# Retention attention and an ELU feed-forward on one core: chunks of 64 tokens on 64x64 quads, with keys and values re-laid by DMA, in place of chunks of 128 tokens kept two tokens to a partition

## The chip, the core and the metric

The kernel runs on one core of a Trainium2 chip. The metric is the device time of one execution, in microseconds (us). The profile is of one execution and gives the span from the first to the last instruction, which is a little shorter than the device time.

The core has a matrix engine (PE in the profile, with its weight loads shown apart as PEld), a vector engine (DVE), a scalar engine (ACT), a third elementwise engine (POOL), and a queue processor (SP) that here only issues DMAs. PE multiplies a stationary block (at most 128 by 128) with a moving block of up to 512 columns and writes into PSUM, which has eight banks of 512 fp32 columns. POOL does not read PSUM in this kernel. Three queues can issue DMAs: SP's, POOL's and ACT's.

## What is computed

The inputs are `q`, `k` and `v` (8 batches, 8 heads, 576 tokens, 64 values a head, fp32) and two weights of 512 by 2048 and 2048 by 512. Attention is linear with a decay in place of a softmax, so that it can be computed in chunks with a running state. What follows is a feed-forward network (FFN) on all 4608 tokens.

```python
scores = scale * np.matmul(q, k.transpose(0, 1, 3, 2))
gamma = 1.0 - 2.0 ** (-5.0 - np.arange(H, dtype=np.float32))
rel = pos[:, None] - pos[None, :]
Dmat = np.where(rel >= 0, gamma[:, None, None] ** rel[None, :, :], 0.0)
attn = np.matmul(scores * Dmat, v)            # 8 batches, 8 heads, 576 x 64
x = attn.transpose(0, 2, 1, 3).reshape(B * S, H * D)      # 4608 x 512
h = x @ w_in                                              # 4608 x 2048
g = np.where(h > 0.0, h, np.exp(np.minimum(h, 0.0)) - 1.0)
out = g @ w_out                                           # 4608 x 512
```

## The kernel before

**Decay and chunks.** The decay `gamma ** (i - j)` splits into a factor on the queries and one on the keys (`gq`, `gk`, scaled copies made by `scaled` at L427). Inside a chunk the scores are multiplied by a 0/1 mask; what earlier chunks contribute comes from a state, the sum of `k^T v` over them, kept per head pair as a block-diagonal 128x128 matrix.

**Attention items.** There are 36 items. A main item is 256 tokens of one batch and 4 heads (two items, `w` = 0 and 1, for each batch and each of two `T`), so 32 of them; a tail item holds the last 64 tokens of two batches with all 8 heads, and there are 4 of these. A main item loads q, k and v with 256 KB each, as pairs of neighbouring tokens in one partition (`(p e) d -> p h (e d)`, packets of 512 B). A chunk of a main item is 128 tokens: 64 partitions with two parities `e`. So keys never have to be moved: `do_scores` (L547) makes a 128x128 score block a head out of 64x64 matmuls with 128 columns, in four quadrants of the array at once ("quads"), and `do_values` and `do_state` sum over the two parities.

**From load to x.** For each main item: POOL or DVE scale q and k (four instructions of 128x256), POOL or ACT cast v; q and k are transposed, by PE for the first seven items (`turn_pe`, L449, `PE_TURN = 7`) and after that by a DMA transpose on SP's queue (L491); PE makes scores; DVE multiplies them by the mask (L673, 128x1024); PE adds the values and the part from the states into two banks; ACT or DVE copy these into `xt`, the input of the FFN. The states go from PSUM to `mid` and `end` (L630 to L639, DVE) and POOL spreads them over the block diagonal (L647).

**How PE runs attention.** The first items run in separate pieces (`early`, `early_out`). Then one "stretch" (L738) puts the state part of the previous item, the scores of this one, the values of the previous one and the states of this one behind one another. A stretch reserves two of the six banks of class `f` (`reserve`, L729); the score tile has two banks of its own (`sc`).

**FFN.** It works in 18 blocks of 256 tokens. FFN1 (`ffn1`, L801) fills one bank with 8 matmuls of 256 columns; ACT takes the exponential, DVE (or ACT) the middle step, DVE makes `g`. FFN2 (`ffn2`, L853) sums 16 matmuls of 512 columns into one bank for 128 tokens; ACT copies it and SP stores it. FFN1 of one block is interleaved with FFN2 of the block before.

**The order of the work** is made when the program is built: `Plan` (L35) is a list scheduler with a cost for every step, with slots for tiles and banks, and with a model of the DMA queues. Each engine executes its steps in the order that the plan gives. `rank` is the priority, and `LEAD = 64` puts attention four blocks ahead of the FFN. The weights come by POOL's queue, cast to bf16 on the way, in four pieces each (L406, L414).

Of the kernel before, what the change touches and what calls it, by code (L numbers as in the profile page):

```python
# [22 lines left out]
class Op:  # L23


    def __init__(self, name, cost, deps, emit, rank, take=(), use=(), banks=(), dma=None, after=None):
# [5 lines left out]
        self.slot, self.waits = {}, []  # L32


class Plan:  # L35
# [30 lines left out]
    def run(self, began):  # L66
# [29 lines left out]
        def pick(e, now):  # L96
            best = None
            for op in ready[e]:
                if best is not None and best[0] <= op.rank:
                    continue  # L100
# [12 lines left out]
                if got is not None:  # L113
                    best = op.rank, op, got
            return best
# [5 lines left out]
        for e, t in began.items():  # L121
            heapq.heappush(events, (t, next(count), None))
        now = 0.0
        while len(order) < len(self.ops) or any(wire.values()) or events:
# [37 lines left out]
            heads = {e: h for e, h in heads.items() if h[3] or big in ([], [e])}  # L162
# [23 lines left out]
ENTER, LEAVE = 1.25, 0.55  # L186


LEAD = 64
HOLD = {}  # L190
RANKS = {}
TOGETHER = 1
EARLY = 5
LOOSE = True
LASTB = 15
ORDER = (0, 1, 2, "t0", 3, "t1", 4, 5, 6, "t2", 7, "t3")
PE_TURN = 7
WG = ("ck11", "ck11", "ck11", "ck12")
WOG = ("ck13", "ck13", "ck13", "ck13")
FREE = ("f", "e", "em", "g", "ot")  # L200

SLOTS = {
    "f": 6, "sc": 1,
    "rqk": 8, "rv": 8, "qkn": 5, "vn": 6, "qkT": 5, "pt": 3,
    "rqt": 4, "rvt": 2, "qkt": 4, "vt": 2, "qkTt": 4, "ptt": 2,
    "xt": 5, "g": 20, "e": 4, "em": 4, "ot": 5, "mid": 4, "end": 4, "s_mid": 4, "s_end": 16,
# [4 lines left out]
def kernel(  # L211
# [15 lines left out]
    FT = 4  # L227
    ST = 64
    NU = FT + 1
    KJ = DM // P  # L230
    NFT = DF // P
    TB = 256
    NP = NFT // 2
    MID = S // 2
    C = 64
    assert (DM, S, D, HP) == (H * D, FT * P + ST, 64, KJ)

# [19 lines left out]
    for h in range(H):  # L257
        nc.vector.memset(lgt[:, h : h + 1], lg[h])
    pos_i = const.tile([P, NU], I32, name="pos_i")
    nc.gpsimd.iota(pos_i[:, :FT].rearrange("p (t e) -> p t e", e=2), pattern=[[2 * P, 2], [1, 2]], base=-MID,  # L260
                   channel_multiplier=2)
    nc.gpsimd.iota(pos_i[:ST, FT:], pattern=[[0, 1]], base=FT * P - MID, channel_multiplier=1)
    nc.gpsimd.iota(pos_i[ST:, FT:], pattern=[[0, 1]], base=MID - FT * P, channel_multiplier=-1)
    pos = const.tile([P, NU], FP32, name="pos")
# [5 lines left out]
    bt = const.tile([P, 1], FP32, name="bt")  # L270
    nc.vector.memset(bt[:ST], math.log(scale))
    nc.vector.memset(bt[ST:], 0.0)
    expo = const.tile([P, NU, H], FP32, name="expo")
    nc.vector.tensor_tensor(
        expo,
        pos.unsqueeze(2).to_broadcast([P, NU, H]),
        lgt.unsqueeze(1).to_broadcast([P, NU, H]),
        ALU.mult,
    )
    gq = const.tile([P, NU, H], FP32, name="gq")  # L280
    nc.scalar.activation(gq[:, :FT], expo[:, :FT], AF.Exp, bias=bq)
    nc.scalar.activation(gq[:, FT], expo[:, FT], AF.Exp, bias=bt)
    gk = const.tile([P, FT, H], FP32, name="gk")
    nc.scalar.activation(gk, expo[:, :FT], AF.Exp, bias=bk, scale=-1.0)

    mask = const.tile([P, 2, 2, C], BF16, name="mask")
    nc.vector.memset(mask, 1.0)
    for c in range(2):
        for ek in range(2):
            for eq in range(2):  # L290
                m = mask[c * C : (c + 1) * C, ek, eq]
                nc.gpsimd.affine_select(out=m, in_=m, compare_op=ALU.is_ge, fill=0.0, base=eq - ek,
                                        pattern=[[2, C]], channel_multiplier=-2)
    mask_t = const.tile([P, ST], BF16, name="mask_t")
    nc.vector.memset(mask_t, 1.0)
    for c in range(2):
        m = mask_t[c * ST : (c + 1) * ST]
        nc.gpsimd.affine_select(out=m, in_=m, compare_op=ALU.is_ge, fill=0.0, base=0, pattern=[[1, ST]],
                                channel_multiplier=-1)
    diag = const.tile([P, 2], FP32, name="diag")  # L300
    nc.gpsimd.memset(diag, 0.0)
    nc.gpsimd.memset(diag[:D, :1], 1.0)
    nc.gpsimd.memset(diag[D:, 1:], 1.0)
# [3 lines left out]

    plan = Plan(SLOTS)  # L310
# [8 lines left out]
    holds, chain = [], {}  # L319
# [4 lines left out]
    items = []  # L324
    for b in ORDER:
        for r in range(FT if isinstance(b, int) else 1):
            it = Item()
            it.tail = not isinstance(b, int)
            if it.tail:
                it.half = int(b[1]) % 2  # L330
                it.b, it.blk = 2 * int(b[1]), "AB"[int(b[1]) // 2]
            else:
                it.b, it.T, it.w = b, r // 2, r % 2
                it.blk = 2 * b + it.T
            items.append(it)
    for n, it in enumerate(items):
        it.n = n
        it.early = n < FT
    at = {(it.b, it.T, it.w): it for it in items if not it.tail}

    seq = list(range(2 * B))
    seq = [*seq[:B], "A", *seq[B:LASTB], "B", *seq[LASTB:]]
    place = {blk: i for i, blk in enumerate(seq)}
    for it in items:
        it.rank = it.n * 4 - 64 if it.early else place[it.blk] * 16 - LEAD + 6 * (it.half if it.tail else it.w)

    def load_main(it, srcs="qkv"):
        n = it.n  # L350
        if not hasattr(it, "ld"):
            it.ld = {}
# [68 lines left out]
    def scaled(it, i, e, cost):  # L421
# [8 lines left out]
        if first:  # L430
            it.cq = {}
# [562 lines left out]
```

## Time and profile before

| | us |
|---|---|
| device time, 3 runs | 309.63, 310.08, 311.87 |
| device time, median | 310.08 |
| span of the profiled execution | 307.9 |
| PE busy | 294.6 (96%) |
| DVE, ACT, POOL busy | 218.0, 153.4, 148.3 |
| FFN1 matmuls, 1152 with 256 columns: busy | 147.5 |
| FFN2 matmuls, 546 with 512 columns (30 more are not in the records): busy | 138.0 |
| mask on DVE, 32 with 128x1024: busy, mean of one | 38.9, 1.215 |

The span of 307.9 us and the median of 310.08 us differ by 2.2 us, which is what an execution spends outside its first and last instruction; this is taken as fixed below. A time in the profile counts from the first instruction. "Busy" is the time in which at least one instruction of a group was under way; since matmuls overlap in the pipeline, the cost of one is read from the distance of two starts and not from its own duration. An entry such as `f<-xt,w_in_sb` names the tile written and the tiles read. A "releaser" is what ended the idle time ahead of an instruction.

### The profile page before, as it was taken

Reading aid. Unit: us, or ns where it says so; the run is one execution under the profiler, and the core shown is the slowest. Engines: PE = TensorE matmul, PEld = TensorE weight load, DVE = VectorE, ACT = ScalarE, POOL = GpSimd, SP = SyncE. Lnnn points to the kernel's source line nnn. Section 1 sums busy time; section 2 is a strip of 40 time slices with the busy share of each in tenths; the row PEclk is TensorE's granted clock in tenths of the full one; section 3 lists DMA queues with packets and bytes.
Section 4 is the critical chain, followed back from the end, with each engine's and each line's share of the span. In section 5 each row is a group of like instructions: output and inputs, shape, how many; then the busy total and the mean of one; then the engine's idle time right before and its main releaser. Section 6 shows DMA issues by size and latency. Waiting matters only on the chain.

```text
span 307.9 us, 8903 instructions
## 1 busy us (share of the span) xinstructions
PE 294.6 (96%) x3600; PEld 207.0 (67%) x3647; DVE 218.0 (71%) x395; ACT 153.4 (50%) x297; POOL 148.3 (48%) x258
## 2 busy tenths in 40 slices
PE   7789999999999999999999999999999999999995
PEld 3576747767677676676676676667776666666654
DVE  4997835887687878888778787667676666666650
ACT  3467815565556645554545545345446343444431
POOL 5983469958876779988776775003011000000000
PEclk9999999999999999999999999999999999999999
DMA  6999999999999999999999998101011010000122
GB/s 198 271 216 216 216 270 256 263 249 211 247 231 211 217 247 277 243 247 305 247 214 212 274 221 151 36 35 38 34 36 36 35 36 34 36 34 34 39 56 78
DMA packets 103768, 50.12 MB, mean 163 GB/s; under 512 B 45744, under 2 KB 99248, under 8 KB 103728
## 3 DMA queue, kind: packets, MB, share of 16 engines
q1 hardware_dynamic: 99504, 45.37, 69.9%
q0 software_dynamic: 4224, 4.19, 8.0%
q8 instruction: 28, 0.46, 0.6%
q14 instruction: 12, 0.10, 0.1%
HBM read 36.70 MB, written 9.44 MB: 150 GB/s over the span
## 4 chain that ended last, share of the span: by engine, by line
PE 86%; DMA 10%; issue 2%; DVE 1%; POOL 1%; ACT 0%
PE f L245 81%; DMA rqk<-in_q_dram 6%; DMA rqk<-in_k_dram 4%; PE sc L245 3%; PE f L455 1%; POOL qkn L427 0%; PE f L953 0%; DVE qkT L461 0%; POOL s_end L647 0%; DVE qkn L427 0%; ACT ot L872 0%; DVE s_end L647 0%; DVE zero L250 0%; DVE end L639 0%
## 5 line engine op out<-in xcount | busy, mean ns | idle before, releaser
L245 PE MATMUL f<-xt,w_in_sb 128*128 128x256 bf16 x1152 | 147.5, 273 | 0.1
L245 PE MATMUL f<-w_out_sb,g 128*128 128x512 bf16 (+1 forms) x546 | 138.0, 373 | 4.3 <-issue 3.0
L817 ACT ACTIVATE e<-f 128x512 f32<-128x512 f32 x144 | 86.0, 597 | 109.2 <-PE f L245 107.5
L245 PEld LDWEIGHTS <-w_in_sb 128*128 128x128 bf16 x1152 | 111.5, 98 | 38.0
L831 DVE TENSOR_SCALAR em<-e 128x512 bf16<-128x512 f32 x105 | 53.3, 508 | 49.9 <-ACT e L817 49.3
L245 PEld LDWEIGHTS <-g 128*128 128x128 bf16 x592 | 56.0, 98 | 39.4
L841 DVE SCALAR_TENSOR_TENSOR g<-f,em 128x512 bf16<-128x512 f32 x105 | 72.2, 688 | 9.1 <-DVE em L831 0.5
L647 POOL TENSOR_TENSOR s_mid<-mid,diag 128x256 bf16<-128x256 f32 x32 | 20.0, 624 | 51.2 <-ACT mid L630 24.6
L427 POOL TENSOR_TENSOR qkn<-rqk,gq 128x256 bf16<-128x256 f32 x61 | 37.6, 632 | 11.6 <-DMA rqk<-in_q_dram 7.6
L427 POOL TENSOR_TENSOR qkn<-rqk,gk 128x256 bf16<-128x256 f32 x59 | 38.4, 667 | 5.3 <-DMA rqk<-in_k_dram 5.1
L673 DVE TENSOR_TENSOR pt<-sc,mask 128x1024 bf16<-128x1024 f32 x32 | 38.9, 1215 | 1.7 <-PE sc L245 1.7
L839 DVE SCALAR_TENSOR_TENSOR g<-e,f 128x512 bf16<-128x512 f32 x39 | 26.1, 682 | 6.0 <-ACT f L827 6.0
L872 ACT COPY ot<-f 128x512 f32<-128x512 f32 (+1 forms) x36 | 20.6, 575 | 17.8 <-PE f L245 17.7
L708 ACT CAST xt<-f 128x256 bf16<-128x256 f32 x50 | 20.0, 450 | 10.8 <-PE f L245 10.2
L827 ACT ACTIVATE f<-f 128x512 f32<-128x512 f32 x36 | 21.4, 595 | 0.0
L443 POOL CAST vn<-rv 128x512 bf16<-128x512 f32 x28 | 17.6, 629 | 7.4 <-DMA rv<-in_v_dram 7.3
L647 POOL TENSOR_TENSOR s_end<-end,diag 128x256 bf16<-128x256 f32 x28 | 17.4, 623 | 4.2 <-DVE end L639 2.7
L245 PE MATMUL sc<-qkT 64*64 64x128 bf16 x512 | 13.4, 222 | 1.7 <-DVE qkT L461 1.6
L245 PE MATMUL f<-pt,vn 64*64 64x128 bf16 x512 | 12.7, 217 | 0.0
L245 PEld LDWEIGHTS <-qkT 64*64 64x64 bf16 x512 | 8.2, 106 | 5.4 <-DVE qkT L461 2.2
L506 POOL TENSOR_TENSOR qkt<-rqt,gq 128x256 bf16<-128x256 f32 x16 | 9.9, 638 | 3.0 <-DMA rqt<-in_k_dram 3.0
L461 DVE COPY qkT<-f 128x512 bf16<-128x512 bf16 x11 | 4.6, 421 | 9.4 <-PE f L455 9.4
(65 smaller groups left out, 139.4 us busy)
## 6 DMA issues: line engine op xcount, KB each, us to landing
rqk<-in_q_dram SPq DMA_DIRECT2D x32, 256.0 KB, 5.1
rqk<-in_k_dram SPq DMA_DIRECT2D x32, 256.0 KB, 5.2
rv<-in_v_dram SPq DMA_DIRECT2D x32, 256.0 KB, 5.0
out_dram<-ot SPq DMA_DIRECT2D x31, 256.0 KB, 3.7
w_in_sb<-in_moe_w_in_dram POOLq DMA_DIRECT2D x4, 512.0 KB, 12.6
w_out_sb<-in_moe_w_out_dram POOLq DMA_DIRECT2D x4, 512.0 KB, 19.3
out_dram<-ot SPq DMA_DIRECT2D x10, 128.0 KB, 2.4
rqt<-in_q_dram SPq DMA_DIRECT2D x8, 128.0 KB, 4.0
```

What stands on the lines that cost most here:

```text
L245: pin(nc.tensor.matmul(*a, **kw))
L427: pin(alu[op.eng].tensor_tensor(tiles[key][:, i, e], tiles[raw][:, :, e], g, ALU.mult))
L443: pin(copy[op.eng](tiles["vn", n], tiles["rv", n]))
L647: pin(alu[op.eng].tensor_tensor(tiles[key].rearrange("p h (j d) -> p h j d", j=2), tiles[src].unsqueeze(2).to_broadcast([P, 2, 2, D]), dia ...
L673: pin(nc.vector.tensor_tensor(tiles["pt", n].rearrange("p i h n -> p (i h) n"), tiles["sc", n].rearrange("p i (h n) -> p (i h) n", h=2), m ...
L708: pin(copy[op.eng](dst, src))
L817: pin(nc.scalar.activation(tiles[ekey], tiles[hkey], AF.Exp))
L827: pin(nc.scalar.activation(ph, ph, AF.Relu))
L831: pin(alu[op.eng].tensor_scalar_add(em, e, -1.0))
L839: pin(nc.vector.scalar_tensor_tensor(g, e, -1.0, ph, ALU.add, ALU.min))
L841: pin(nc.vector.scalar_tensor_tensor(g, ph, 0.0, tiles["em", blk, p], ALU.max, ALU.min))
L872: pin(copy[op.eng](tiles[okey][:, :width], tiles[pkey][:, :width]))
```

## The change

The attention part is built anew, and the FFN's blocks are made wider. The scheduler gets an earliest time for a step (`early`), a `gate` on reservations, and lets ACT's queue run beside POOL's.

- A main item is 256 tokens of one batch with all 8 heads, so 16 of them; a tail item is 64 tokens of four batches, so 2. Chunks have 64 tokens. q, k and v still come as pairs of tokens; after scaling and casting into a staging tile `kvs`, two DMAs an item (`re0`, `re1`, 256 KB each) lay keys and values out again as one token a partition (`kvn`). For the first three items ACT's queue issues them, after that SP's.
- Scores, values and states are 64x64 matmuls with 64 columns, 32 of each an item. The state part has 16 matmuls an item, 128x128 with 64 columns.
- The first five items (40 heads x 256 tokens; before: the first seven, 28 heads x 256 tokens) are transposed by PE; from there on q goes by one DMA transpose and k by two, these after the re-laying.
- All eight PSUM banks are of class `f`. A stretch reserves six of them: two for scores, two for x, two for states. Masks are two of 128x512 an item; states are summed one after another over four chunks (128x256) and put on the block diagonal by two copies each into a ring of zeroed tiles.
- FFN: four blocks with 256 tokens, then seven with 512, so that FFN1 has 448 matmuls with 512 columns and 256 with 256. The weights come in 9 pieces (the first two of `w_in` half as large), at times written down in `AT`.

```diff
-LEAD = 64
-EARLY = 5
-PE_TURN = 7
-WG = ("ck11", "ck11", "ck11", "ck12")
-WOG = ("ck13", "ck13", "ck13", "ck13")
+SW_ENTER = 4.4
+LEAD = 96
+EARLY = 5
+ACT_LAY = 3
+PE_TURN = 5
+AT = {"wi0": 9.6, "wi1": 10.4, "wi2": 11.2, "wi3": 13.0, "wi4": 15.0, "wo0": 17.0, "wo1": 19.0, "wo2": 22.0, "wo3": 25.0}
+NBD = 8
+SURE = 3
+ATT = ((0, 0), (0, 1), (1, 0), (1, 1), (2, 0), (2, 1), (3, 0), (3, 1), (4, 0), (4, 1), "X",
+       (5, 0), (5, 1), (6, 0), (6, 1), (7, 0), (7, 1), "Y")
+FFN = (((0, 0),), ((0, 1),), ((1, 0),), ((1, 1),), ((2, 0), (2, 1)), ((3, 0), (3, 1)), ((4, 0), (4, 1)),
+       ((5, 0), (5, 1)), ((6, 0), (6, 1)), ("X", "Y"), ((7, 0), (7, 1)))
+W_IN = ((0, 1), (1, 2), (2, 4), (4, 6), (6, 8))
...
-    "f": 6, "sc": 1,
+    "f": 8, "rq": 3, "rk": 3, "rv": 3, "qn": 3, "kvs": 3, "kvn": 3, "qT": 3, "kT": 3, "pt": 2,
+    "xt": 4, "g": 33, "e": 4, "em": 4, "ot": 5, "S": 4,
...
+        for s in range(2):
+            def emit(op, s=s):
+                eng = nc.scalar if op.eng == "ACT" else nc.sync
+                pin(eng.dma_start(tiles[nkey][:, s].rearrange("p i h d -> p (i h d)"),
+                                  tiles[skey][s * C : (s + 1) * C].rearrange("p e i n -> p e (i n)")))
...
+            op = add(f"re{s}_{n}", {"ACT": 0.5} if n < ACT_LAY else {"SP": 0.5}, [*it.ck.values(), *it.cv], emit,
+                     it.rank if n < ACT_LAY else -1, use=[skey, *use], dma=(0.75, 8), **kw)
...
+                for s in range(2):
+                    def emit(op, tkey=tkey, s=s):
+                        pin(nc.sync.dma_start_transpose(tiles[tkey][:, s],
+                                                        tiles[nkey][:, s, 0].rearrange("p h d -> p (h d)")))
...
+    def do_scores(it):
+        kt = tiles["kT", it.n]
+        for hp in range(HP):
+            for s in range(2):
+                for par in range(2):
+                    for i in range(2):
+                        part = slice(i * D, (i + 1) * D)
+                        sc = tiles["sc", it.n, i].rearrange("p (h s n) -> p h s n", h=HP, s=2)
+                        mm(pairs(sc[rows(par), hp, s]), kt[part, s, hp, rows(par)], queries(it, part, hp, s, par),
+                           start=True, stop=True)
...
+    def do_inter(it, xkey):
+        for s in range(2):
+            for par in range(2):
+                state = state_of(it, 2 * s + par)
+                if state is not None:
+                    for hp in range(HP):
+                        acc((xkey, par), 2, pairs(quad(xkey, par, s, hp)), tiles[state][:, hp],
+                            queries(it, slice(0, P), hp, s, par))
...
+        def gate():
+            if any(r.start is not None for r in mine):
+                return True
+            free = sum(old is None or plan.left[old] == 0 for old in plan.slots["f"])
+            return free >= len(keys) or any(
+                f[0].start is not None and sum(x.start is None and all(d.done is not None for d in x.deps) for x in f) >= SURE
+                for f in tilesof2)
...
+        st = add(f"A{it.n if it else 'last'}", {"PE": cost}, deps, emit, (it or prev).rank - 4, use=use)
+        reserve(st, ([("sc", it.n, i) for i in range(2)] if it else []) + (banks_of(xkey) if prev else [])
+                + (banks_of(tkey) if it and not it.tail else []))
...
-    def ffn1(blk, p, rank):
+    def ffn1(blk, p, rank, after):
+        per, first = 512 // blk.w, blk.i < 2
+        fts = range(per * p, per * (p + 1))
...
+            for f, ft in enumerate(fts):
                 for j in range(KJ):
-                    mm(ph[:, f * TB : (f + 1) * TB], w_in_sb[:, j, ft * P : (ft + 1) * P], xt[:, j],
+                    mm(ph[:, f * blk.w : (f + 1) * blk.w], w_in_sb[:, j, ft * P : (ft + 1) * P], xt[:, j],
                        start=(j == 0), stop=(j == KJ - 1))
```

The deps of a stretch are the masks, the states and the re-laid tiles of the previous item, and the transposed and re-laid tiles of this one. For the first five items `early` runs scores, states and outputs as three separate pieces.

## The prediction

> **What bounds the kernel now.** I read the page's busy slices first, then the chain, then busy times by stage, then single stretches of PE's timeline.
>
> ```profile
> PE   7789999999999999999999999999999999999995
> ...
> DMA  6999999999999999999999998101011010000122
> ```
> ```profile
> 18.76:47.17 28.41, 26.80 (x297) 18.97 (x292) 19.83 (x37) 17.44 (x35) 15.10 (x26) 1.00 1.20 233
> 47.17:304.50 257.33, 253.00 (x3043) 178.63 (x3085) 184.42 (x316) 127.60 (x246) 118.14 (x195) 1.00 0.73 152
> ```
>
> The slices are 7.7 us each: PE is full from the fourth on, DMA only up to the 25th. The second view has stretch, length, then busy time of PE, PEld, DVE, ACT and POOL, clock, DMA share and GB/s. The first FFN1 matmul starts at 18.76 us, the last FFN2 matmul ends at 304.5. Between them PE is the bound at a granted clock of 1.00; DVE has 72% of the long stage, ACT 50%. "PE 86%" in the chain says the same. So time comes off only as PE work, or as the head before 18.76 us.
>
> What PE's time consists of is read from starts:
>
> ```profile
> 257.45 1.04 PE L245 MATMUL f<-xt,w_in_sb 128*128 128x256 bf16 x8
> 258.33 1.03 PE L245 MATMUL f<-w_out_sb,g 128*128 128x512 bf16 x4
> 259.19 1.04 PE L245 MATMUL f<-xt,w_in_sb 128*128 128x256 bf16 x8
> ```
>
> Eight FFN1 matmuls take 0.875 us (109.4 ns each), four FFN2 matmuls 0.865 (216 ns each; starts to another digit are from the same records). The whole FFN is 1152 x 0.1094 + 576 x 0.2163 = 250.6 us, of the 285.7 between 18.76 and 304.5. The other 35 us are attention and a little idle time. Two stretches of attention:
>
> ```profile
> 85.92 0.40 PE L245 MATMUL f<-qkTt,s_end 128*128 128x64 bf16 x8
> 86.25 0.42 PE L245 MATMUL sc<-qkT 64*64 64x128 bf16 x16
> 86.50 0.29 PE L245 MATMUL f<-ptt,vt 64*64 64x64 bf16 x16
> 86.62 0.30 PE L245 MATMUL f<-vn,qkn 64*64 64x64 bf16 x16
> 86.86 0.39 PE L245 MATMUL f<-xt,w_in_sb 128*128 128x256 bf16 x2
> ```
> ```profile
> 117.51 0.28 PE L245 MATMUL f<-qkT,s_mid 128*128 128x128 bf16 x2
> 117.71 0.42 PE L245 MATMUL sc<-qkT 64*64 64x128 bf16 x16
> 117.96 0.39 PE L245 MATMUL f<-pt,vn 64*64 64x128 bf16 x16
> 118.18 0.29 PE L245 MATMUL f<-vn,qkn 64*64 64x64 bf16 x16
> 118.41 0.83 PE L245 MATMUL f<-xt,w_in_sb 128*128 128x256 bf16 x6
> ```
>
> Sixteen quad matmuls take 0.25 us with 128 columns and 0.12 with 64. A 128x128 matmul with 64 columns starts every 0.029 us (inside the 85.92 group). Each stretch also pays some 0.09 us on entering the quads and 0.12 on leaving. A stretch is 0.90 us with two state matmuls; two more, at 56 ns each, make 1.01; a tail's is 0.80 (105.34 to 106.14).
>
> **The change, part by part.**
>
> *Attention on PE, steady form.* Before: 16 x 0.90 + 16 x 1.01 + 4 x 0.80 = 33.8 us. After, a main item: 16 state matmuls 0.47 + 0.09, 32 score matmuls 0.25, 32 value matmuls 0.25, 32 state-making matmuls 0.25, leaving 0.12: 1.43. Behind a batch's first item four state matmuls fall away: 1.31. A tail item has no state-making: 1.18. Sum 8 x 1.43 + 8 x 1.31 + 2 x 1.18 = 24.3 us, 9.5 less. What runs before FFN1 starts isn't on the path: before, some 3.5 items (3.4 us); after, 1.5 of the doubled items (2.1 us). So 9.5 - 1.3 = 8.2 off the path.
>
> The row under this is 16 quad matmuls with 64 columns in 0.12 us, 8 ns each. The Trainium skill (TensorEngine Tiling (Array Packing), Instruction Overhead) says that each matmul carries some 60 cycles, so that tiling should not be taken from a dimension that is already small. Counted once a quad, this agrees with the 31 ns that four take; as a price a matmul it is the third rival.
>
> *More transposes and pieces in the head.* PE transposes 80 blocks instead of 56. Of these 24 and some 54 lie after FFN1's start; at 56 ns (a 128-column matmul) that adds 1.7 us. Items run as three pieces pay entry and exit twice more, 0.4 us: about 3.5 of them after the start against one now, so +1.0.
>
> *FFN1 with 512 columns.* 448 matmuls at 0.2163 replace 896 at 0.1094: -1.1 us.
>
> So far: -8.2 + 1.7 + 1.0 - 1.1 = -6.6 us on PE.
>
> *Six banks for a stretch.* This wait is new. Now a stretch takes two of six banks and two of its own; afterwards it waits until six of eight are free, and queued behind it on PE is all of the FFN, while ACT (exponentials) and DVE wait for PE's banks. A FFN1 bank is held through matmuls 0.87, exponential 0.60, middle step 0.51 and `g` 0.69, so some 3 us; the plan opens the reservation when six banks are free or three FFN2 pieces (2.6 us) are ready as cover. What is uncovered is at least 0, and at most some 0.9 us a stretch (3.5 with DVE's queue, less 2.6). For 13 stretches: 0 to 12 us. I take 0.15 each, 2 us, nearer to 0, since in the long stage of before (257.3 us, 30 reservations) FFN takes 228.9 (250.6 less the 21.7 done by 47.17, which is 28.4 less 6.7 of attention and transposes) and attention about 28, so that no idle time can be told.
>
> *DVE, ACT and POOL* are off the path and stay so. DVE: masks fall from 32 x 1.215 + 4 x 0.68 to 36 x 0.68 (-17 us); state sums go from 64 of 0.28 to 64 of some 0.42 (twice the columns), +9; x copies 72 x 0.45 become 36 of 0.45 to 0.9, most on ACT. POOL's scaling is the same elements (120 x 0.65); the block diagonals 64 x 0.62 stay near 64 x 0.7. If this cover were gone, `g` would come late and PE with it.
>
> *The re-laying.* 36 new DMAs of 256 KB from SBUF to SBUF. No row shows one. Nearest: DMAs of 256 KB land 0.67 (store), 0.9 (load) and 0.9 us (transpose) after the one before, where the queue is full; beside the streaming weights a load takes 3.7. I take 0.7, the row with the same 2 KB rows; 0.5 to 3.7 stays as range. Per 256 tokens DMA then needs 6 x 0.9 + 2 x 0.7 + 1.9 (transposes) + 1.3 (stores) = 10 us, against 15.3 us of PE (13.9 FFN + 1.4): hidden, with DMA idle later than the 192 us of now. SP issues them in line: behind each wait loads, transposes and stores; a load queue that lives on being ahead covers this. Cost 0; without cover, below.
>
> *The head.* FFN1 starts now on the first `w_in` piece (issued 9.3, landed 8.5 us later, at 17.8). Half a piece lands earlier by half of the 3.7 us that pieces are apart, near 16. But x now needs six loads (the sixth lands at 9.3), casts, re-laying (about 3.5 us), a chain of three state sums at 0.42, a block diagonal, values and a copy: about 17.5. I take no change; -1.5 to +5 us. POOL and DVE also zero eight tiles there (some 0.3 us each).
>
> *The tail* (last FFN2, copy, store: 3.4 us) is as it was: 0.
>
> **Sum.** Span 307.9 - 6.6 + 2 = 303.3; with 2.2 us outside the span 305.5, against the median of 310.08: 1.5% less. Ends of its own unknowns: 302 (no bank wait, early head) to 309.
>
> **The rivals.**
>
> *Banks eat the gain.* PE waits 0.6 us at each of 13 stretches: +8 in place of +2, so 311.5, within 1%. For it: six of eight banks, and after a stretch DVE owes 2 x 0.68 and 4 x 0.42, 3 us, while FFN work queues behind. Against: FFN2 needs one bank for 3.5 us of work, and `g` is held a block ahead. The Trainium skill (Perfetto Trace Analysis, Optimization Strategy) says that a gap repeating on the engine that should be saturated can mean too little PSUM for the next tile. That gap is what this rival would show; the trace of before has none.
>
> *The re-laying meets the weights.* This ends slower. Weights stream from about 14 to 43 us, and loads then come every 3.7 us:
>
> ```profile
> 34.55 1.18 POOL L427 TENSOR_TENSOR qkn<-rqk,gk 128x256 bf16<-128x256 f32 x2 [2.04 <-DMA rqk<-in_k_dram]
> 38.22 0.61 POOL L443 CAST vn<-rv 128x512 bf16<-128x512 f32 x1 [2.49 <-DMA rv<-in_v_dram]
> 42.00 0.61 POOL L427 TENSOR_TENSOR qkn<-rqk,gq 128x256 bf16<-128x256 f32 x1 [1.75 <-DMA rqk<-in_q_dram]
> ```
>
> If a re-laying takes a load's turn there, the second block's x comes at 17 + 2 x 3.7 + 5, some 29 us in place of 25, and the weights end some 4 us later. PE then has one block's FFN1 (7 us from 17.5) and idles about 4 us; item 2 is late by as much, and the first 512-token block, which needs items 4 and 5 complete (I count 82 to 86 us, PE out of other work at 86 to 89), stalls 4 to 6 more. 305.5 + 9 = 314.5. It decides from about 2 us for each of the first six re-layings. For it: DMA's share is full in the head. Against: other queues take turns beside each other, and 256 KB in 2 KB rows is little.
>
> *Quads gain nothing from 64 columns.* If each 64-column quad matmul cost alone what four of them now take together, 31 ns, the 1664 of them (16 x 96 + 2 x 64) would take 23 ns more each, +38, so 343 us. That is the rule of the Trainium skill named above, read as a price a matmul. The 0.12 us groups speak against it; the sixteen at 86.50 are this very instruction.
>
> **How the numbers follow.** Forecast 0.53, banks 0.18, re-laying 0.27, quads 0.02. Faster by over 1% (about what a measurement can tell from no change) means under 307.0; slower means over 313.2. Of the forecast's 302 to 309 I put 0.49 under 307 and 0.04 above; of the banks 0.01 under 307 (half the wait), 0.14 within and 0.03 slower; of the re-laying 0.25 slower and 0.02 within; the quads are slower. Together: faster 0.50, same 0.20, slower 0.30. The range leaves out the quads, the worst of the re-laying and the best of the head: 300.5 to 317; the forecast alone is 302 to 309.
>
> **What would show it.** Right: stretches of 1.3 to 1.45 us on PE, about 24 us of attention, FFN1 512-column starts 216 ns apart, PE full after 47 us, DMA full beyond 192. Banks: idle PE ahead of scores or the FFN matmul behind them, ended by DVE or ACT. Re-laying: FFN1 after 20 us, or PE waiting for `kvn` before 90 us. Wrong: a PE that waits elsewhere, or re-layings that land over 2 us apart.

## The result, and the profile after

The changed kernel takes 354.75 us (median; 354.28 to 356.08), the kernel before 310.07 (309.63 to 311.87) beside it: a ratio of 1.145, 95% interval 1.141 to 1.149, so 44.7 us slower. Its profiled execution has a span of 353.0 us. The forecast was 305.5, and the range ended at 317. Times are medians over all executions of a kernel; the ratios leave out two of them (one of e3, one of e5), which took over 1.5% longer than the fastest of the same kernel.

The same rows of the page as before the change, in slices of 8.8 us, with the clock that PE was granted and what DMA moved:

```profile
PE   8380089989999999899299999977999999999996
...
PEclk9857579999999999999769999999999999999999
DMA  8999963219999999999999999999800110011122
GB/s 218 276 224 223 243 158 62 62 61 261 285 219 251 264 245 240 174 198 270 224 255 230 227 223 236 233 252 171 185 32 30 48 43 30 32 48 42 32 59 89
```

PE does next to nothing in the fourth and fifth slice, where before it was full from the fourth on, and it has holes again in slices 20, 27 and 28. DMA is busy until the 29th slice, but nearly empty from the seventh to the ninth. The same two stages as before (stretch, length, busy time of PE, PEld, DVE, ACT and POOL, clock, DMA share, GB/s):

```profile
18.76:47.17 28.41, 9.57 (x140) 8.85 (x141) 5.39 (x13) 2.11 (x4) 6.64 (x11) 0.62 1.18 233
47.17:349.50 302.33, 284.00 (x3158) 156.36 (x3186) 195.16 (x356) 159.34 (x285) 125.18 (x206) 0.98 0.75 157
```

In the first stage PE has 9.6 us of work where it had 26.8, and most of that is not FFN work but filler on zeros. The long stage is 302 us where it was 257. What PE and ACT did there, by their timelines (start, length, what; in brackets the idle time before and what ended it):

```profile
26.49 0.61 PE L253 MATMUL f<-zero 128*128 128x128 bf16 x8
45.52 2.72 PE L253 MATMUL f<-xt,w_in_sb 128*128 128x256 bf16 x12 [18.42 <-ACT xt L667]
```
```profile
24.41 0.82 ACT L632 CAST bd<-S 64x256 bf16<-64x256 f32 x2
37.18 7.52 ACTq L473 DMA_DIRECT2D kvn<-kvs  x2
44.75 0.72 ACT L667 CAST xt<-f 128x512 bf16<-128x512 f32 x1 [19.52 <-DMA rv<-in_v_dram]
47.42 0.60 ACT L774 ACTIVATE e<-f 128x512 f32<-128x512 f32 x1 [1.96 <-PE f L253]
```

FFN1 starts at 45.52 us in place of 18.76. It waits for ACT's half of the copy of block 0's x; the values of that block were done at 26.3. ACT did nothing in between: it stood at the issue of item 1's two re-layings (ACTq, L473), from 25.2 to 37.18 at the first and to 44.17 at the second, and the copy was behind them in its order. The DMA records say which completion semaphore each transfer of SP's and ACT's queues signals. There are eight numbers, and every issue waits until the last transfer with its number has landed:

```
issued  semaphore  landed  queue  transfer
 16.49     105      37.09  SP     q of item 2, second half
 26.22     107       -     SP     v of item 3, second half (landing not in the records)
 37.18     105      43.75  ACT    re-laying of item 1, first half
 44.17     107       -     ACT    re-laying of item 1, second half
```

The keys were ready by 23 us (the same issue comes then in a later run); the semaphores were not. Loads landed 3.65 us apart at that time, beside the weights. The damage goes on at SP:

```profile
41.42 3.42 SPq L368 DMA_DIRECT2D rv<-in_v_dram  x2
44.96 0.72 SPq L368 DMA_DIRECT2D rk<-in_k_dram  x1
73.64 0.84 SPq L842 DMA_DIRECT2D out_dram<-ot  x2
```

After 45.7 us the next in SP's order is the first store of an output. FFN2 is late by then, so SP issues nothing for 28 us, and that is the DMA hole at 62 GB/s. Attention then is late and has its stretches at fixed places in PE's order:

```profile
PE f L253 <- ACT xt L667: 18.4, 1, 18.4
PE f L253 <- POOL bd L632: 8.2, 5, 6.1
PE f L253 <- DMA kvn<-kvs: 7.3, 3, 4.9
PE f L253 <- DMA kT<-kvn: 5.8, 7, 2.2
```

These are PE's waits (for what; total, times, longest): 18.4 us ahead of FFN1 and, earlier still, most of the 7.3 for re-laid tiles; then 14 us for block diagonals and transposed keys, late in the kernel. The stretch itself is about what was forecast:

```profile
198.12 0.51 PE L253 MATMUL f<-qT,bd 128*128 128x64 bf16 x12
198.56 0.45 PE L253 MATMUL f<-qT,kT 64*64 64x64 bf16 x32
198.84 0.46 PE L253 MATMUL f<-pt,kvn 64*64 64x64 bf16 x32
199.12 0.50 PE L253 MATMUL f<-kvn 64*64 64x64 bf16 x32
199.55 1.04 PE L253 MATMUL f<-xt,w_in_sb 128*128 128x512 bf16 x3
```

From 198.12 to 199.55 are 1.43 us, with no wait for banks.

### The profile page after: what moved, and what is told of

Read it like the earlier page. It is cut to its first block, busy times and chain, and to the rows that moved or that the text cites. A ratio compares the mean times of both kernels' runs of the same rounds, so it can differ in the third digit from the quotient of the medians.

```text
span 353.0 us, 8616 instructions
## 1 busy us (share of the span) xinstructions
PE 304.2 (86%) x3454; PEld 173.3 (49%) x3485; DVE 208.6 (59%) x401; ACT 165.8 (47%) x297; POOL 139.5 (40%) x238
## 4 chain that ended last, share of the span: by engine, by line
PE 52%; DMA 22%; SPq 10%; POOL 7%; issue 3%; DVE 3%; ACT 2%; ACTq 0%; POOLq 0%; DVEq 0%
PE f L253 50%; DMA rv<-in_v_dram 9%; DMA rk<-in_k_dram 4%; DMA kT<-kvn 4%; SPq L368 3%; POOL bd L632 3%; DMA rq<-in_q_dram 3%; SPq L525 2%; POOL qn L438 2%; DMA kvn<-kvs 2%; SPq L517 2%; SPq L473 1%; POOL kvs L438 1%; SPq L373 1%; PE f L917 1%
## 5 line engine op out<-in xcount | busy, mean ns | idle before, releaser
L253 PE MATMUL f<-xt,w_in_sb 128*128 128x512 bf16 (+1 forms) x691 | 142.3, 343 | 19.0 <-ACT xt L667 18.4
L253 PEld LDWEIGHTS <-w_in_sb 128*128 128x128 bf16 x704 | 68.4, 99 | 75.8 <-issue 19.2
L632 POOL CAST bd<-S 64x256 bf16<-64x256 f32 x114 | 47.8, 419 | 59.3 <-DVE S L615 29.5
L788 DVE TENSOR_SCALAR em<-e 128x512 bf16<-128x512 f32 x87 | 42.2, 486 | 45.6 <-ACT e L774 45.5
L667 ACT CAST xt<-f 128x512 bf16<-128x512 f32 x34 | 22.7, 734 | 53.3 <-PE f L253 33.8
L438 POOL TENSOR_TENSOR kvs<-rk,gk 128x512 bf16<-128x512 f32 (+1 forms) x34 | 33.0, 984 | 35.0 <-DMA rk<-in_k_dram 30.7
L643 DVE TENSOR_TENSOR pt<-f,mask 128x512 bf16<-128x512 f32 x36 | 23.1, 684 | 24.2 <-PE f L253 24.2
L438 POOL TENSOR_TENSOR qn<-rq,gq 128x512 bf16<-128x512 f32 (+1 forms) x35 | 32.8, 952 | 10.7 <-DMA rq<-in_q_dram 9.6
L615 DVE TENSOR_TENSOR S<-f,S 128x256 f32<-128x256 f32 x56 | 23.5, 420 | 3.5
L455 POOL CAST kvs<-rv 128x512 bf16<-128x512 f32 x25 | 14.8, 618 | 8.5 <-DMA rv<-in_v_dram 8.1
L253 PEld LDWEIGHTS <-kvn 64*64 64x64 bf16 x1088 | 12.5, 108 | 8.7 <-DMA kvn<-kvs 7.7
L253 PEld LDWEIGHTS <-bd 128*128 128x128 bf16 x256 | 10.4, 99 | 12.7 <-POOL bd L632 8.9
```

Of the source, the lines that this page charges most:

```text
L253: pin(nc.tensor.matmul(*a, **kw))
L438: pin(alu[op.eng].tensor_tensor(dst, tiles[src][:, hs, e], g, ALU.mult))
L615: pin(nc.vector.tensor_tensor(tiles[skey], st_ap(), tiles[prev[1]], ALU.add))
L632: pin(copy[op.eng](tiles[bkey][part, :, part], tiles[skey][part]))
L643: pin(nc.vector.tensor_tensor(tiles["pt", n][:, i].rearrange("p h s n -> p (h s) n"), tiles["sc", n, i].rearrange("p (h n) -> p h n", n=C) ...
L667: pin(copy[op.eng](dst[:, par], src))
```

## The experiments

To see where a kernel falls behind, I add up its FFN matmuls by their starts (109.7 ns for 256 columns, 216.3 for 512, scaled to 250.6 us where records are missing). The runs are told one after the other below; this is the table that they lead to:

| kernel | time, us | first FFN1 | FFN done by 48 us | by 80 us | from 80 to 272 us |
|---|---|---|---|---|---|
| before | 310.07 | 18.76 | 22.2 | 48.9 | 168.6 |
| changed | 354.75 | 45.52 | 1.4 | 23.6 | 148.4 |
| e1, ACT freed | 339.22 | 25.99 | 14.3 | 33.0 | 154.2 |
| e3, re-laying on SP | 345.94 | 21.25 | 13.3 | 33.1 | 152.4 |
| e7, e3 with honest DMA costs | 326.77 | 23.17 | 14.2 | 32.3 | 170.0 |
| e9, ACT freed and honest costs | 328.32 | 25.28 | 10.1 | 31.6 | 167.1 |
| e16, as e9, re-laying for items 0 to 4 and the tails only | 325.66 | 26.38 | 8.8 | 31.0 | 170.2 |
| e15, re-laying from item 5 on only | 315.66 | 16.24 | 18.6 | 41.1 | 170.5 |
| e13, none: one-token loads | 309.24 | 16.05 | 20.6 | 44.9 | 173.2 |
| e11, none: left out | 308.42 | 16.89 | 22.1 | 46.1 | 173.6 |

The changed kernel is 25.3 us of FFN work behind by 80 us, and loses 20.2 more until 272: together the 45 us. "Ratio" below is to the kernel before on the same chip, with its 95% interval.

### First round: is it the issue on ACT, or the transfer?

**e1: ACT freed.** Two loads are ordered behind the re-laying that ACT issues, by a copy of one column on ACT into the tile that they load (the changed kernel has such a mechanism, with POOL, and doesn't use it: its line `HOLD = {}` is not among the lines of the diff ahead of the prediction):

```diff
-HOLD = {}
+HOLD = {(2, "q"): "re1_1", (3, "v"): "re1_2"}
...
-            if n in HOLD and s == "q":
+            if (n, s) in HOLD:
...
-                    pin(nc.gpsimd.memset(tiles[key][:, 0, 0, :1], 0.0))
+                    pin(nc.scalar.copy(tiles[key][:, 0, 0, :1], zero[:, :1]))
```

> The edit orders two loads behind the re-laying that ACT issues (q of item 2 behind item 1's, v of item 3 behind item 2's), so that the re-laying's completion semaphores are those of loads long landed. Theory (queue): ACT stood from 18.4 to 44.75 us because the issue of item 1's re-laying waited for loads that share its two semaphores, with the copy of block 0's x and the exponentials behind it. Then the first FFN1 matmul comes by 28 us in place of 45.5 (DVE's half of that copy ended at 27.1), item 1's re-laying is issued before 26 us, and the time is 313 to 324 us. Rival (slow transfers): the re-laying itself, 6.6 to 7.4 us from issue to landing beside the weights, holds up the head; then FFN1 still starts after 38 us and the time stays over 340. Second rival (banks): with the head mended PE still idles some 0.6 us at each stretch after 60 us, and the time is 324 to 335.

339.22 us, ratio 1.091 (1.086 to 1.097). ACT's timeline:

```profile
23.20 0.53 ACTq L473 DMA_DIRECT2D kvn<-kvs  x1
23.71 0.39 ACT L632 CAST bd<-S 64x256 bf16<-64x256 f32 x1
23.77 0.62 ACTq L473 DMA_DIRECT2D kvn<-kvs  x1
24.11 0.40 ACT L632 CAST bd<-S 64x256 bf16<-64x256 f32 x1
25.07 0.73 ACT L667 CAST xt<-f 128x512 bf16<-128x512 f32 x1 [0.56 <-PE f L253]
```

The issue comes at 23.20 in place of 37.18, the copy at 25.07 in place of 44.75, and FFN1 starts at 25.99. The mechanism of the head holds; the time does not: 15 us came back, not the 31 to 42 of the expectation. PE's waits in this run are for re-laid tiles (10.8 us), block diagonals (7.5) and transposed keys (5.0), and none is for a bank, so banks are not it either. The second hold also left SP without work from 29.8 to 53.9 us, which no theory had foreseen.

**e2: only item 1's re-laying freed**, with the mechanism that was there: `HOLD = {2: "re1_1"}`.

> Only item 1's re-laying is freed; item 2's, on ACT too, still shares its semaphores with loads of item 3. Theory (queue): FFN1 starts by 28 us as with both freed, but ACT stands a second time, some 4 to 9 us between 36 and 50 us, behind item 2's re-laying, and the time is 4 to 10 us over that of the kernel with both freed. Rival (slow transfers): no difference between the two, both over 340.

340.97 us (one run). ACT doesn't stand a second time: item 2's re-laying is only reached at 47.88, when its semaphores are free. So the 4 to 10 us over e1 that the theory gave this kernel didn't come (1.8 us). Item 1's re-laying is issued at 23.01, when its data are ready, with the weights beside it as before and on semaphores of loads that landed by 15.34. In the changed kernel the issue came 0.09 us after the load with its number had landed. So it is the semaphore that the issue waited for, and not the traffic.

**e3: all re-layings on SP's queue**, `ACT_LAY = 0`.

> All re-layings go to SP's queue, so that nothing on ACT waits for a DMA's semaphore. Theory (queue): FFN1 starts by 30 us; SP now stands until the first items' casts are done and the loads of items 2 to 4 come later, so 316 to 332 us. Rival (slow transfers): the re-layings land no sooner, FFN1 after 38 us, over 340.

345.94 us, ratio 1.110 (1.102 to 1.117). FFN1 starts at 21.25, as the queue theory has it, and yet the time is 14 us over its range. The rival has the time right and the reason wrong. A third thing is at work.

**e4: weights 12 us later**, every time in `AT` raised by 12.

> The nine weight pieces are issued 12 us later each, with the re-layings where they were: the price of the stream of weights beside them. Item 0's two re-layings took 6.6 and 7.4 us from issue to landing. Rival (slow transfers): that is the weights' share, and without them they take under 4.5 us. Theory (queue): the loads that item 1's re-layings wait for land by some 22 us, so it is issued by 24 us in place of 37 and 44; FFN1 is then bound by the first weight piece, some 30 to 33 us; time 318 to 338.

342.13 us (one run). The re-layings issued at 11.80, 23.51 and 24.08 landed 7.9, 6.8 and 7.3 us later, though POOL issued the first weights only at 29.25. So the rival's reason falls: the weights are not what makes a re-laying slow, loads on SP's queue are enough. Where SP had nothing under way (e1, issued 48.16) one landed after 3.2 us. Item 1's was issued at 23.51, as the queue theory says; FFN1 came at 44.1, later than expected, and the time is 4 us over the theory's range. The first weights had landed at 35.4, but in PE's fixed order the states of item 2 stand ahead of FFN1, and these waited for re-laid tiles until 41.4.

### Second round: the re-laying, its bytes, the order

**e5: no re-laying.** Transposes, values and states read the staging tile, which gets the six slots that it and the re-laid tile had between them. The kernel so leaves out putting keys and values into the order that the result needs, and serves for its time alone:

```diff
-        it.laid = []
-        for s in range(2):
...
-            it.laid.append(op)
+        it.laid = [*it.ck.values(), *it.cv]
```

> The 36 re-layings are left out: transposes, values and states read the staging tile itself, of the same size, so keys and values stand in the wrong order; all other work is that of the changed kernel. Theory (DMA bound): with both ACT's and SP's waits for them gone and 9.4 MB less to move, at the 235 GB/s of the full stage some 40 us of DMA, the last transpose lands by 205 us in place of 256, FFN1 starts at 17 to 21 us, and the time is 302 to 312 us, near the sum of the prediction. Rival (the rest of the rebuilding costs: six-bank stretches, wide blocks, state sums): 320 or more, with PE idle at the stretches all the same.

313.29 us, ratio 1.005 (1.000 to 1.011). The re-laying is worth some 41 of the 44.7 us, with everything that hangs on it. FFN1 starts at 18.07, the last transpose lands at 190 us.

**e6: the bytes in the kernel before**, for every main item a transfer that nobody needs (into a tile of its own with three slots):

```diff
+        def emit_lay(op):
+            pin(nc.sync.dma_start(tiles["lay", n], flat(n)))
+
+        add(f"lay{n}", {"SP": 0.5}, list(it.cq.values()), emit_lay, -1,
+            take=[T("lay", ("lay", n), [P, 1024], BF16)], use=[("qkn", n)], dma=(0.75, 8))
```

> The kernel before with 32 transfers of 256 KB from SBUF to SBUF put on SP's queue, one an item ahead of its transpose, into a tile that nobody reads: the bytes of the re-laying without its waits. Theory (DMA bound): DMA is full until 192 us before; 8.4 MB more at 239 GB/s move its end to some 225 us, PE then waits for items, and the time is 318 to 335 us. Rival (the bytes are hidden, only the waits for the re-laid tiles cost): 308 to 313 us.

314.14 us, ratio 1.010 (1.007 to 1.014). DMA's last transpose moved from 192 to 221 us, as expected, and PE hardly noticed: 3.5 us. My theory that DMA's bytes bound the kernel falls. Five of these copies were issued by 31 us, and by 80 us the FFN work done is 47.5 us against 48.9: also in the head the bytes cost little as long as nothing waits for them. One caution: these copies landed 0.68 us apart (median), the re-layings of e3 1.0, so they are a cheaper transfer of the same size.

**e7: honest DMA costs.** On top of e3, the planner is told 1.13 times the cost of every transfer but the weights; no work and no transfer is added or taken away. The plan changes the order, and with it which of ACT, DVE and POOL does some of the elementwise steps:

```diff
-                        wire[e].append([enter, op.dma[0], op, False])
+                        wire[e].append([enter, op.dma[0] * (1.0 if e == "POOL" else 1.13), op, False])
```

> As with all re-layings on SP's queue, and the planner is told 1.13 times the cost for every transfer on SP's queue, so that the plan's last transpose lands at 235 us (real: 231) in place of 207; no transfer is changed. Theory (order): what was lost after 28 us is PE standing in a fixed order that was made for faster DMA; with FFN work put where attention really comes late, 318 to 328 us. Rival (DMA's bytes alone bound it): 338 to 346 as before.

326.77 us, ratio 1.054 (1.050 to 1.058): 19 us less than e3 for an order. In the table the loss after 80 us is gone (170.0 against 168.6 before), the one in the head is not. There PE's longest waits are now for pieces of `w_out`:

```profile
PE f L253 <- DMA w_out_sb<-in_moe_w_out_dram: 6.5, 4, 2.8
```

These pieces land less than 2 us later than in the kernel before (34.2 to 45.1 us against 32.3 to 43.3). PE has come to them early, with no other work ready.

**e8: blocks of 256 tokens**, on top of e3: `FFN = tuple((key,) for key in ATT)`, six slots of `xt`.

> As with all re-layings on SP's queue, with the FFN in 18 blocks of 256 tokens again (six slots of xt in place of four). Theory (wide blocks): a block of 512 tokens needs two items, and two of them come after the last item, so with narrow ones PE has work while it waits and the time is 325 to 336 us against 346. Rival (DMA and order): 342 to 350, no more than some 1 us for FFN1's narrower matmuls.

343.73 us (one run), which is among the times of e3 (341.6 to 347.3). The wide blocks are not the cause.

### Third round: both repairs, and the two controls

**e9: e2's hold on q of item 2 (by ACT's copy) and e7's costs**, re-layings where the change has them.

> The changed kernel with two repairs and no work changed: item 2's q load is ordered behind item 1's re-laying on ACT (so that no re-laying waits for a late load's semaphore), and the planner is told 1.13 times the cost of the transfers on SP's and ACT's queues. Theory (queue and order): freeing ACT alone gave 339, the honest order alone (with the re-layings on SP) 327; together FFN1 starts at 23 to 28 us and goes on, and the time is 314 to 323 us. Rival (the two repairs mend the same thing): 325 to 330.

328.32 us, ratio 1.053 (1.047 to 1.060): the rival. The two repairs don't add up; with either placement an honest order gives 327 to 328.

**e10: in the kernel before, the transposes read e6's copy**, so that each waits for a landing in SP's line.

> As in the kernel before with the 32 added transfers, but the DMA transposes now read the copy that the transfer made, so that each stands behind its transfer's landing, with SP waiting for it in line; the output is unchanged. Bytes alone cost 3.5 us. Theory (waits in SP's line): the transposes and all that is queued behind them come some 4 to 5 us later an item, DMA idles meanwhile, and the time is 318 to 335 us. Rival (a chain longer by one transfer is covered by the load's lead): 312 to 317.

315.42 us, ratio 1.011 (1.004 to 1.018). Also the wait behind a landing is covered there, by loads that are items ahead. This is a test of the later items only: the first seven are transposed by PE in that kernel and don't read the copy.

**e11: e5 with the planner told 1.08 times the DMA costs.**

> The re-layings are left out as before, and the planner is told 1.08 times the cost of the transfers on SP's queue. Theory (order): the 313 us without re-layings still held some 8 us of PE waiting in an order made for faster DMA, so 303 to 309 us, near the 305.5 of the prediction's sum. Rival (bank waits and state sums): 311 to 315 again.

308.42 us, ratio 0.991 (0.988 to 0.995): without re-laying the rebuilt attention is 1% faster than before. (Like e5, it leaves out the order of keys and values.) The other 20 us (328.3 against 308.4) then go with the re-laying and are not ACT's stand. How much of them is one order against another, e17 lets guess.

### Fourth round: where the last 20 us are

**e12: first stores planned later** (66 and 74 us), on top of e9: `.early = (66.0, 74.0)[blk.i] if blk.i < 2 else 0.0` on the store.

> As the kernel with both repairs (328.3 us), and the first stores of the FFN's output are planned no earlier than 66 and 74 us, so that SP's line has loads and item 3's re-layings ahead of them. There SP stood from 48.7 to 62.3 us behind the first store, which waits for FFN2. Theory (stores at the head of SP's line): that stand goes, DMA is full between 48 and 64 us in place of 110 GB/s, and the time falls by 4 to 13 us, to 315 to 324. Rival (DMA's hole is made up later, FFN in the head is what is late): 326 to 330.

329.25 us, ratio 1.058 (1.053 to 1.064): no gain, though DMA moved 152 GB/s between 48 and 64 us in place of 110. In this kernel SP's stand behind the store goes with the late FFN and is not what costs the time.

**e13: one-token loads.** The whole function without re-laying: k and v are loaded with one token a partition, in runs of 256 B, and the keys get a decay table for that order (1.08 in the planner, 1.2 us a load). As in e5, the staging tile has six slots:

```diff
+                    if src is not q:
+                        half = slice(0, P) if c is None else slice(c % 2 * C, c % 2 * C + C)
+                        for s in (hs,) if c is None else (c // 2,):
+                            lo = TB * it.T + (s * P if c is None else 0)
+                            b, n = (it.b, P) if c is None else (it.b + c, C)
+                            pin(nc.sync.dma_start(tiles[key][half, :, s],
+                                                  src[b, :, lo : lo + n, :].rearrange("h p d -> p h d")))
...
+    nc.gpsimd.iota(pok_i[:, :4], pattern=[[P, 4]], base=-MID, channel_multiplier=1)
...
+    nc.scalar.activation(gk, expok, AF.Exp, bias=bk, scale=-1.0)
```

> No re-laying at all, with the result kept: k and v are loaded with one token a partition (runs of 256 B in place of 512), with the keys' decay for that order; 128 KB loads of such runs landed 0.7 to 0.8 us apart in the kernel before, so 1.5 us for 256 KB against 0.9. Theory (the waits, not the bytes): DMA has some 2.4 us more an item than without re-laying, and no wait; FFN1 starts at 17 to 20 us and the time is 308 to 318 us. Rival (DMA's time alone decides, and short runs cost as much as the re-laying): 322 to 335.

309.24 us, ratio 0.995 (0.991 to 0.998): 45 us better than the changed kernel, and half a per cent better than the one before. Its page, in slices of 7.7 us:

```profile
PE   8979999999999999999999999999999999999995
...
DMA  8999999999998999999999999999410001011131
```

PE is full from the fourth slice, though DMA is full until the 28th (217 us), 25 us longer than in the kernel before. Loads of 256 KB landed some 1.1 us apart (k and v, median) against 0.93 for q, with runs of 512 B, in the same run: about 20% more, where I had feared 65%. The Trainium skill (DMA: Bandwidth & Descriptors, Why small descriptors are slow) puts the fixed overhead of a packet of 256 B at 27%. By the same sum (3 cycles beside one for every 32 B) a packet of 512 B has 16%, which makes an estimate of 16% more time for the same bytes; the trace is near it.

**e14: the same with blocks of 256 tokens** and the planner told 1.5 us a load (factor 1.0).

> The same, with FFN blocks of 256 tokens and the planner told 1.5 us for such a load in place of 1.3. Theory (wide blocks need two items, and with late attention narrow ones leave PE work): 1 to 6 us less than with wide blocks. Rival: within 1 us of them.

313.95 us, ratio 1.011 (1.007 to 1.015). 4.7 us worse: neither expected. Block width and planner costs changed together, so the run doesn't tell which.

**e15: one-token loads for items 0 to 4 only**, where PE does the transposes (planner 1.13 as in e7 and e9): `it.one = n < EARLY`.

> Only the first five items load k and v with one token a partition and have no re-laying; items 5 to 17 are re-laid on SP's queue as in the changed kernel. The planner is told 1.13 times the DMA costs, as in the two kernels at 327 and 328 us, which had done 32 us of FFN work by 80 us (before: 49) and lost nothing more after. Theory (the rest is the head: items 0 to 4 each wait 6 to 8 us for their re-laying): FFN work of 42 to 48 us by 80 us, and 308 to 316 us in all. Rival (DMA time of the late re-layings, with DMA full to 241 us): 322 to 329.

**e16: the complement**, `it.one = n >= EARLY and not it.tail`, with e9's hold.

> The complement: items 0 to 4 and the two tail items are re-laid (the first three on ACT, with the q load of item 2 ordered behind), the other main items load k and v with one token a partition; planner as before. Theory (head): 30 to 34 us of FFN by 80 us, and 322 to 330 us as with all items re-laid. Rival (late re-layings): 308 to 316.

315.66 us, ratio 1.014 (1.008 to 1.020), and 325.66, ratio 1.046 (1.040 to 1.053). Both as the theory of the head has it: to take away the first five items' re-layings is worth 12.7 us against e9, to take away the later ones 2.7. PE's waits in e9 name the place; it has four waits for re-laid tiles, all before 36 us:

```profile
PE f L253 <- DMA kvn<-kvs: 8.1, 4, 3.8
PE f L253 <- DMA kT<-kvn: 3.0, 5, 1.1
```

**e17: e13 with another guess of the costs** (factor 1.0, 1.3 us a load).

> One-token loads for all items with wide blocks as in the kernel at 309.2 us, with another guess of the planner's DMA costs (1.3 us for a load of k or v, factor 1.0, in place of 1.2 and 1.08). Theory (order): within 2 us of it either way, since both plans end their transposes at 208 to 216 us; more than 4 us apart would speak for an order that is sensitive to single places.

320.39 us, ratio 1.029 (1.022 to 1.037): 11 us worse than e13 by nothing but the plan. That is a warning for everything above: a fixed order made from guessed costs moves this kernel by 10 us, so the share of the order (11 us from e1 to e9, 19 from e3 to e7) is a size and not a number, and so are the single microseconds of e12 to e16. The signs of the large steps stand: e1 and e2 against the changed kernel, and the head: six kernels without re-laying there (e5, e11, e13, e14, e15, e17) take 308 to 320 us, in six orders, and none with it takes less than 325 (medians). The three pairs that differ in the planner's costs alone (e3 and e7, e5 and e11, e17 and e13) all gained from higher ones, by 19, 5 and 11 us.

## Why the prediction was wrong, by its steps

**What failed: "The re-laying ... Cost 0" and "The head ... I take no change; -1.5 to +5 us".** The two terms were costed apart, as 0.7 us of DMA time each and as "re-laying (about 3.5 us)" in item 0's chain. Measured: 6.6 and 7.4 us from issue to landing for item 0, FFN1 26.8 us later. Three things were missing. First, it was known that ACT's queue issues the first three items' re-layings (the section on the change says so), but the prediction reckons only with SP's line. It doesn't ask what stands behind them on ACT (block 0's copy and all exponentials), nor whether an issue waits for the completion semaphore of an earlier transfer; that alone is 14 to 15 us of the 44.7 (e1, e2). Second, a load that lands late was taken to delay only its own item; but PE's order is fixed when the program is built, with DMA costs below the real ones, so a late item stops FFN work that was ready: 11 to 19 us (e7, e9). Third, a re-laying in the head is one more transfer in series, 6 to 8 us beside loads, for each of the first items: about 13 us (e15, e16). The three sizes each rest on one or two orders, so they are rough, and that they add up to about 44.7 is not a proof of each.

**The rival "re-laying meets the weights"** had the right place and the right signs to look for: FFN1 after 20 us (45.5), PE waiting for `kvn` before 90 us (it did). Its price was wrong: 9 us for 44.7. It counted the turns of transfers beside the weights, and e4 shows that the weights aren't even needed for it. "It decides from about 2 us for each of the first six re-layings" was right, and they took more than three times that.

**What held: PE's sum.** Stretches were forecast at 1.31 and 1.43 us and are 1.43 and 1.55 (209.06 to 210.61) where nothing in them waits: 0.12 too little each, some 2 us over 16 items. 512-column matmuls are 216 ns apart. The six-bank wait, taken as 2 us with 12 as its end, is not to be seen: none of PE's long waits in the changed kernel is for a bank, which settles the rival "banks eat the gain", and the 1.43 us settle "quads gain nothing". Take the re-laying away and the sum of 305.5 us meets 308.4 (e11) and 309.2 (e13). These are the best orders found: e5 takes 313.3 and e17 320.4 with the same work on PE, so it is partly luck that they come so near.

**DMA.** "DMA full beyond 192" came true (29 slices, 256 us), and "hidden" did too in its narrow sense: e6 and e10 put as many bytes, and then the wait, into the kernel before, for 3.5 and 4 us. Per transfer 0.7 us was too little: the re-layings landed 1.0 us after the transfer before (median, in the changed kernel and in e3). The sentence "a load queue that lives on being ahead covers this" was true of the later items (2.7 us, e16 against e9) and not of the head, where nothing is ahead.

**The chances.** 0.30 was given to slower. The profile of before could have said more: it shows loads landing 3.65 us apart until 43 us, and 512 KB of SBUF traffic an item was put into just that stage, in front of PE's first work.

## What to carry to other kernels

Before a DMA is given to a computing engine's queue, list what that engine has to do behind it, and ask which earlier transfer its issue can wait for: here eight completion semaphores, shared by two queues, turned a transfer that was costed at nothing into a wait for somebody else's load. In this kernel a transfer in series at the start was paid for (about 13 us), and the same one behind a lead of several items was nearly free (2.7 us); so cost it by place and not by bytes. And where the order is fixed by a planner, feed it measured transfer times, and take differences under 10 us between two orders as luck until a third order agrees.

## What was not expected of the hardware

**The clock follows the holes.** In e9 PE was idle from 13.55 to 17.36 us. The granted clock, by half microseconds (stretch, length, PE busy, clock, DMA share, GB/s):

```profile
16.50:17.00 0.50, 0.00 (x0) 0.94 1.22 280
17.00:17.50 0.50, 0.14 (x12) 0.50 1.17 237
...
23.00:23.50 0.50, 0.50 (x11) 0.50 1.19 216
23.50:24.00 0.50, 0.50 (x25) 0.73 1.21 219
24.00:24.50 0.50, 0.50 (x37) 1.00 1.23 233
```

It halves 3.4 us after the last matmul and comes back some 5 us after PE is busy again (at 18.6; 3.3 us in the changed kernel after 45.5). The Trainium skill (TensorE: Matmul & The Clock Gate, Part 1: The HAM clock gate) gives a window of about 3.4 us for each of the two edges; the fall agrees, and the return took about one to two such windows here. In the changed kernel the two long holes cost work at half speed after them as well: 45.5 to 48.8, and 175.2 to 181.9 us. The head of e9 paid in the same way (mean clock 0.57 from 16 to 24 us and 0.51 from 34 to 41), that of e15 didn't (1.00 in both), so a part of the 13 us between them is the clock; how large a part no run separates.

**A second queue buys latency.** Item 1's first re-laying landed 6.7 us after its issue on ACT's queue (e2), and 19.1 us after it on SP's, behind loads (e7, issued 14.39, landed 33.45). The Trainium skill (DMA: Bandwidth & Descriptors, Issuing engines are not separate DMA queues) says that several issuing engines only save time on the sequencer. The same page (Queues, rings and completion order) has each DMA engine go round between the queues, which agrees with the 6.7 us. So a second queue hardly moved more bytes here (230 GB/s from 16 to 40 us in e2, 225 in e7), but a transfer on it didn't stand behind those queued on the first.
